# Hh blocks and gz pieces turned through DRAM ahead of their use, product sums ordered later, one w1 gradient piece moved

## The chip, the core and the metric

One Trainium2 chip, one of its cores. The metric is device time in microseconds (us) of one execution. The kernel computes in a single launch.

The engines named below: PE is TensorE, which multiplies matrices; DVE is VectorE; ACT is ScalarE; POOL is GpSimd; SP is SyncE. In this kernel SP and POOL issue all transfers between device memory (DRAM) and on-chip memory (SBUF). Each engine runs its own instructions in order, so an instruction that waits holds up those behind it on the same engine. SP's queue includes the transposing transfers (`dma_start_transpose`), which read a matrix from DRAM and leave its transpose in SBUF. POOL's queue has only plain and indexed transfers.

## The reference

The reference is the forward pass of one conditioned block and all its gradients. With S = 2048 tokens, D = 1024 and F = 3584:

```python
sa, ca, ga, sb, cb, gb = six rows of silu(c) @ w_mod
h = layernorm(x) * (1 + ca) + sa
x = x + ga * irfft2(rfft2(h) * (w_r + 1j * w_i))      # mixer over tokens and channels
h = layernorm(x) * (1 + cb) + sb
x = x + gb * (gelu(layernorm(h) @ w1 + b1) @ w2 + b2) # channel MLP
...
out, vjp = jax.vjp(forward, A_x, A_w_r, A_w_i, w1, b1, w2, b2, c, w_mod)
return out, *vjp(grad_out)
```

Ten outputs: the result, and the gradients of x, w_r, w_i, w1, b1, w2, b2, c and w_mod. The gradient of w2 is the product of the activated hidden values (Hh in this text, transposed) with gB, the output gradient scaled by gb. The gradient of w1 is the product of the normalized input with gz, the gradient at the hidden layer before its activation.

## The kernel before

The transforms are done as matrix products with cosine and sine matrices. All large products run on PE in 128x128 by 128x512 steps of bf16. The tokens are cut into NB = 4 blocks of BW = 512, the hidden size into NFC = 28 pieces of 128 rows (fc), or 7 groups of four (g). In order of time the kernel runs

1. the modulation rows, the product of the output gradient with w2 (ph) and the forward spectral part;
2. the MLP's forward pass (z_block, bo_pass). It also forms gz and stores Hh and gz to DRAM as d_hh and d_gz, both laid out hidden row by token;
3. the gradient passes: for each block b, two passes pg_pass(b, h) of 7 x 16 matmuls (L1083) that read gz (tiles gzr, eight slots filled by load_gz, L1059) and the transposed w1. They are followed by the layernorm backward on DVE and ACT (ln_bwd), the product pru of gradient and n2u (L192), and the column sums of both (sums3, L215) on PE. The block's gradient gn3 becomes d_gx in DRAM, issued on POOL (L1289), and is folded into fbuf for the spectral part. n3u, n2u and au are one-block loads on SP (L1244, L1246, L1299); n2u is then scaled by ACT (L507);
4. the backward spectral part (spectral_core), whose steps are pu (L524, L530), pcs (L569), pv (L639, L655) and po (L737), with DVE work (pairs) between them. PE's holes here are filled with pieces of the w2 gradient: gw2_product, one piece being 16 matmuls (L1214) for half of one fc. Each fc needs its block of Hh with the hidden index along the free side, so hh_load (L1371) loads it with a transpose from d_hh. From fc 8 on three slots serve in turn, and block fc + 2 is asked for when piece fc begins;
5. the four output quarters (consume_bwd), DVE work that ends in out_1, with pieces of the w1 gradient between them and after them (L1409). One piece is again 16 matmuls, and 8 pieces use one group of 512 gz rows, loaded with two transposes (gw1_load, L1360), one group ahead.

The pieces of steps 4 and 5 come from one generator, pieces(), 112 in all less the four done early; fill(n) takes the next n. The calls of fill at fixed places settle how many pieces stand between two steps of the spectral part. In consume_bwd quarter i first gets 6, 6, 8 or 8 pieces, then its column sum (accCA), then 2 more.

The order on each engine is decided by a scheduler at build time from dependences and estimated durations. `tc.issue_after(x)` and `behind(a, b)` are extra rules of order: the first puts what is inside it after x, the second puts a after b on the same engine without a wait. In pg_pass of a block b > 0 the sums of block b - 1 that are in `sums_in` (the first two token rows of both products) are put behind the matmul of step (g, i) = (2, 0):

```python
if b > 0 and h == 0 and (g, i) == (2, 0):
    for ins in sums_in:
        behind(ins, last_pg[0])
    sums_in.clear()
```

The gmod_ring steps (L1123 to L1137) work on the rows of the w_mod gradient beside step 4: loads of w_mod on SP, a reduction and a scaling on DVE, a store on POOL, through three buffers.

Of the kernel before, what the change touches and what calls it, by code (L numbers as in the profile page):

```python
# [11 lines left out]
BF16 = mybir.dt.bfloat16  # L12
# [5 lines left out]
P = 128  # L18
# [3 lines left out]
NT = S // P  # L22
# [9 lines left out]
BW = S // NB  # L32
# [3 lines left out]
def kernel(  # L36
# [24 lines left out]
    nc = tc.nc  # L61
# [4 lines left out]
    reg = ctx.enter_context(tc.tile_pool(name="reg", bufs=1))  # L66
    dram = ctx.enter_context(tc.tile_pool(name="dram", bufs=1, space=bass.MemoryType.DRAM))
# [44 lines left out]
    d_hh = dram.tile([F, S], BF16, name="d_hh")  # L112
    d_gz = dram.tile([F, S], BF16, name="d_gz")
    d_P = dram.tile([8, P, 4 * PW], BF16, name="d_P")
    d_SF = dram.tile([P, 4, 4, 512], BF16, name="d_SF")
    d_SI = dram.tile([P, 2, 4, 256], BF16, name="d_SI")
    d_E = dram.tile([P, 2, 8, 256], BF16, name="d_E")
    d_gmod = dram.tile([6 * D], BF16, name="d_gmod")
    d_ph_v = d_ph.rearrange("(fc p) s -> p fc s", p=P)
    d_hh_v = d_hh.rearrange("(fc p) s -> p fc s", p=P)  # L120
    d_gz_v = d_gz.rearrange("(fc p) s -> p fc s", p=P)
# [390 lines left out]
    def behind(ins, later):  # L512
        tc.add_manual_dep(ins.ins, later.ins.name, mybir.DependencyInfo(mybir.DependencyClass.NoSync, mybir.DependencyReason.DATA),
                          reason="order")
# [534 lines left out]
    gzs, g_sums, gn3s = {}, {}, {}  # L1049

    def gn3_of(b):
        if b % 2 not in gn3s:
            gn3s[b % 2] = reg.tile([P, 4, D], BF16, name=f"gn3{'ab'[b % 2]}", tag=("uv3", "wt")[b % 2])
        return gn3s[b % 2]

    def load_gz(b, g):
        n = b * 7 + g
        gzs[b, g] = gzr[n % 8 // 2][:, n % 2]
        nc.sync.dma_start(out=gzs[b, g], in_=d_gz_v[:, g * 4:(g + 1) * 4, b * BW:(b + 1) * BW])  # L1059

    def behind_w2(k):
        return tc.issue_after(w2_in[(NB - 1) * 14 + min(max(k, 0), 13)].ins)
# [1 line left out]
    for g in range(7):  # L1064
        wtile = reg.tile([P, 4, D], BF16, name=f"w1T_{g}", tag=W1T[g])
        for k in range(4):
            fc = g * 4 + k
# [4 lines left out]
            load_gz(0, g)  # L1072

    last_pg = [None]
    sums_in = []

    def pg_pass(b, h, pool, before=lambda: ExitStack()):
        pgs = [pool(k)("pg") for k in range(4)]
        for g in range(7):
            for i in range(4):  # L1080
                for k in range(4):
                    with before():
                        last_pg[0] = nc.tensor.matmul(pgs[i][:], lhsT=gzs[b, g][:, k, i * P:(i + 1) * P],  # L1083
                                                      rhs=w1Ts[g][:, k, h * KH:(h + 1) * KH],
                                                      start=(g == 0 and k == 0), stop=(g == 6 and k == 3))
                    last_pe[0] = last_pg[0]
                if b > 0 and h == 0 and (g, i) == (2, 0):
                    for ins in sums_in:
                        behind(ins, last_pg[0])
                    sums_in.clear()  # L1090
            for k in range(4 if b < 2 and h == 1 else 0):
                nc.scalar.activation(out=gzs[b, g][:, k, :], in_=gzs[b, g][:, k, :], func=ACT.Identity,  # L1092
                                     accum_out=gb1_acc[:, g * 4 + k, b:b + 1])
            if g < 6:
                yield
        for i in range(4):
            with tc.high_priority():
                nc.scalar.activation(out=gn3_of(b)[:, i, h * KH:(h + 1) * KH], in_=pgs[i][:], func=ACT.Identity,
                                     accum_out=g_sums[b][:, h, i:i + 1])
        yield  # L1100
# [90 lines left out]
    hh_in = [None]  # L1191
# [4 lines left out]
    def sums3(b, g4, p4):  # L1196
        for i in range(4):
            for j in range(4):
                src = (g4, p4)[j // 2][:, i, (j % 2) * KH:(j % 2 + 1) * KH]
                ins = strip_sum(acc3[0], j, src, b == 0 and i == 0, b == 3 and i == 3)  # L1200
                if b < 3 and i < 2:
                    sums_in.append(ins)

    def sums3_ga(b, p4):
        halves_sum(acc3[1], p4, b == 0, b == 3)
# [27 lines left out]
    def fold_quarter(b, ftmp, g2):  # L1233
# [3 lines left out]
        else:  # L1237
            fold2_in[b] = fold_pair(fbuf2[:, b], fbuf2[:, b - 1], ftmp, g2, ftmp[:, 0:2, :])

    for b in range(NB):  # L1240
        if b > 0:
            g_sums[b] = small.tile([P, 2, 4], FP32, name="sums", tag="sums")
# [7 lines left out]
        if b > 0:  # L1250
            for g in range(7):
                load_gz(b, g)
            if b == 2:
                hh_in_frame(0)
                hh_in_frame(1)
            for h in range(2):
                for _ in pg_pass(b, h, lambda k: ps_f):
                    pass
            with tc.issue_after(last_pg[0].ins):
                sums3_ga(b - 1, au)  # L1260
                if b == 2:
                    gb1_rows()
# [57 lines left out]
    hh_s = [hhp[:, 0], hhp[:, 1]] + [otl[:, k * NT * P:(k + 1) * NT * P].rearrange("p (t f) -> p t f", f=P) for k in range(2)] + \  # L1320
        [hht[k // 2][:, k % 2] for k in range(4)]
    hh_o = [None, None] + [4, 5, 6, 7, 4, 5] + [2, 0] + [1, 2, 0] * 6
# [4 lines left out]
    def consume_bwd(i, o4, tmp, tmp2, n1, eb):  # L1327
        if i == 0:
            accCA.append(ps_s("accCA"))
            nc.vector.tensor_copy(out=sacc, in_=eb[:, 0, :])  # L1330
        elif i == 2:
            tt(sacc, sacc, eb[:, 0, :], ALU.add)
        unfold_d(o4, tmp)
        unfold_tok(o4, tmp)
        load_tok(n1, A_x, i, nc.gpsimd)
        with tc.issue_after(last_po[0].ins):
            norm_act(n1, n1, 0, i)
        tt(tmp, o4, n1, ALU.mult)
        s1c = small.tile([P, 4], FP32, tag="s1c")
        for q in range(4):  # L1340
            t = 4 * i + q
            nc.vector.tensor_tensor_reduce(out=o4[:, q, :], in0=o4[:, q, :], in1=opca_row, scale=1.0, scalar=0.0,
                                           op0=ALU.mult, op1=ALU.add, accum_out=s1c[:, q:q + 1])
            ln_bwd(o4[:, q, :], s1c[:, q:q + 1], n1[:, q, :], stats[:, 0, 0, t:t + 1], o4[:, q, :], tmp2[:, q, :])
        nc.sync.dma_start(out=n1, in_=chunk_rows(d_gx1, i))
        tt(o4, o4, n1, ALU.add)
        store_tok(out_1, o4, i)
        fill((6, 6, 8, 8)[i])
        halves_sum(accCA[0], tmp, i == 0, i == 3)
        fill(2)  # L1350
        if i == 3:
            rows = small.tile([P, D], BF16, tag="gmrow", bufs=1)
            store_halves(accCA[0], rows[0:64, 0:KH], tmp, 1)


    w1g = {}

    def gw1_load(fg):
        for k in range(2):
            ins = nc.sync.dma_start_transpose(out=w1g["gz"][2 * (fg % 2) + k][:],  # L1360
                                              in_=d_gz[fg * 512:(fg + 1) * 512, k * 1024:(k + 1) * 1024])
        return ins
# [5 lines left out]

    def pieces():
        def hh_load(fc):  # L1370
            hh_in[0] = nc.sync.dma_start_transpose(out=hh_s[hh_o[fc]], in_=d_hh[fc * P:(fc + 1) * P, :])  # L1371

        for fc in range(2, 6):
            hh_load(fc)
# [45 lines left out]
    def fill(n):  # L1420
        for _ in range(n):
            next(todo)
        done[0] += n
# [86 lines left out]
```

## Time and profile before

| | |
|---|---|
| median of 3 runs | 1435.88 us |
| lowest, highest run | 1435.77, 1447.16 us |
| the profiled execution | 1443.81 us |
| its span, first to last instruction | 1441.9 us |
| mean granted clock of PE | 0.985 |
| moved by transfers | 321.68 MB, mean 223 GB/s |
| packets under 512 bytes | 207210 of 353505 |

How to read what follows. The views of the profile come from that one execution. In the view of stretches, each row gives a stretch of the span, its mean, then for PE, PE's weight loads, DVE, ACT and POOL the busy time with the number of instructions; the last three numbers are the granted PE clock, the share of the transfer engines that was busy (it can pass 1, since packets that wait for each other overlap) and the rate in GB/s. In a timeline, a row is a run of equal instructions: start, time from the first start to the last end, engine, line, operation, tiles; square brackets give the idle time before it and what ended that. In the chain of waits, a row is start, duration and what the end was waiting for at that time. In a list of waits a row names who waited, for whom, the sum in us, how often, and the longest.

### The profile page before, as it was taken

How to read it: one execution, taken by the hardware profiler on the slowest of the kernel's cores; microseconds unless marked ns; L12 is line 12 of the kernel's file. 1: busy time of each engine (PE TensorE's matmuls, PEld its weight loads, DVE VectorE, ACT ScalarE, POOL GpSimd, SP SyncE). 2: the span in 40 equal slices, each digit the busy share in tenths (PEclk: the TensorE clock that was granted, in tenths of full speed). 3: DMA queues.
4: the chain of work that ended last, by engine and by line, in shares of the span. 5: the costliest groups of instructions: out<-in, count | busy, mean ns of one | idle time of the engine just before them, and what ended most of it. 6: DMA issues, size and time to landing. Idle time of an engine off the chain costs nothing. (4 is left out here: it accounts for less than half of the span.)

```text
span 1441.9 us, 18528 instructions
## 1 busy us (share of the span) xinstructions
PE 1369.0 (95%) x6838; PEld 663.5 (46%) x6963; DVE 1072.4 (74%) x1505; ACT 743.9 (52%) x1061; POOL 372.1 (26%) x468
## 2 busy tenths in 40 slices
PE   5999999999999999999999999999997999899996
PEld 2445674444444444444444444444443574444443
DVE  5898889987798886877412999997566859898532
ACT  4775766657987766666117654343422455333111
POOL 5601622201112112221210001202344532232322
PEclk8999999999999999999999999999999999999998
DMA  9963647999687876887998446475999998656993
GB/s 331 296 219 100 171 133 241 270 309 325 204 259 241 244 235 220 253 272 208 307 290 170 146 161 234 168 190 161 231 229 229 251 241 219 194 164 182 280 222 121
DMA packets 353505, 321.68 MB, mean 223 GB/s; under 512 B 207210, under 2 KB 296832, under 8 KB 353286
## 3 DMA queue, kind: packets, MB, share of 16 engines
q1 hardware_dynamic: 317510, 199.84, 53.7%
q0 software_dynamic: 35904, 120.65, 24.8%
q8 instruction: 54, 0.88, 0.3%
q14 instruction: 37, 0.30, 0.1%
HBM read 161.01 MB, written 110.15 MB: 188 GB/s over the span
## 5 line engine op out<-in xcount | busy, mean ns | idle before, releaser
L803 PE MATMUL pp<-gBoT,wt 128*128 128x512 bf16 x874 | 195.2, 379 | 4.5 <-DVE phr L809 1.5
L1083 PE MATMUL pg<-w1T,gzr 128*128 128x512 bf16 x877 | 195.7, 381 | 1.0
L1409 PE MATMUL gw1acc<-gzh,n3n 128*128 128x512 bf16 x876 | 194.2, 379 | 1.1
L1083 PEld LDWEIGHTS <-gzr 128*128 128x128 bf16 x896 | 87.3, 98 | 108.3 <-issue 5.6
L928 PEld LDWEIGHTS <-w 128*128 128x128 bf16 x896 | 87.3, 98 | 107.3 <-issue 2.9
L803 PEld LDWEIGHTS <-wt 128*128 128x128 bf16 x896 | 87.4, 98 | 107.0 <-issue 4.4
L1409 PEld LDWEIGHTS <-n3n 128*128 128x128 bf16 x896 | 87.5, 98 | 104.9 <-issue 1.3
L1214 PE MATMUL gw2acc<-gB,hhsA 128*128 128x512 bf16 x406 | 94.4, 388 | 10.5 <-DMA hhsA<-d_hh 9.8
L928 PE MATMUL pz<-n3Ta,w 128*128 128x512 bf16 x439 | 98.2, 379 | 1.9 <-ACT gt L931 1.5
L928 PE MATMUL pz<-n3Tb,w 128*128 128x512 bf16 x436 | 98.0, 379 | 0.7 <-issue 0.2
L985 PEld LDWEIGHTS <-hhA 128*128 128x128 bf16 x608 | 59.0, 98 | 72.7 <-issue 2.5
L931 ACT ACTIVATE gt<-pz,b_col 128x512 bf16<-128x512 f32 x112 | 73.0, 685 | 34.6 <-PE pz L928 34.2
L1221 ACT CAST gwo<-gw2acc 128x512 bf16<-128x512 f32 x46 | 26.6, 583 | 114.4 <-DMA out_dram<-gwo 50.4
L1413 ACT CAST gwo<-gw1acc 128x512 bf16<-128x512 f32 x47 | 27.4, 584 | 109.8 <-PE gw1acc L1409 98.2
L942 ACT ACTIVATE gt<-gt 128x2048 bf16<-128x2048 bf16 x28 | 53.5, 1910 | 59.2 <-DVE gt L192 59.2
L192 DVE TENSOR_TENSOR gt<-gt,gt 128x2048 bf16<-128x2048 bf16 x56 | 68.5, 1224 | 20.6 <-ACT gt L944 19.4
L192 DVE TENSOR_TENSOR ct<-ct 128x2048 bf16<-128x2048 bf16 x68 | 80.6, 1216 | 3.6 <-DMA d_n<-ct 2.9
L1214 PEld LDWEIGHTS <-hhsA 128*128 128x128 bf16 x416 | 41.2, 100 | 61.0 <-DMA hhsA<-d_hh 11.0
L1134 DVE CUSTOM_DVE_ANT_0 otl<-otl 128x1024 bf16<-128x1024 bf16 x24 | 29.1, 1222 | 51.0 <-DMA otl<-in_w_mod_dram 46.3
L938 ACT ACTIVATE gt<-gt 128x2048 bf16<-128x2048 bf16 x28 | 53.5, 1910 | 1.8 <-DVE w2sA L192 1.0
L944 ACT ACTIVATE gt<-gt 128x2048 bf16<-128x2048 bf16 x28 | 53.4, 1908 | 0.4
L1414 POOL DMA_DIRECT2D out_dram<-gwo x56 | 30.9, 553 | 86.2 <-ACT gwo L1413 44.1
(343 smaller groups left out, 2544.0 us busy)
## 6 DMA issues: line engine op xcount, KB each, us to landing
gzr<-d_gz SPq DMA_DIRECT2D x28, 512.0 KB
wblk<-in_w_mod_dram SPq DMA_DIRECT2D x12, 1024.0 KB
out_dram<-otl POOLq DMA_DIRECT2D x48, 256.0 KB
out_dram<-gwo POOLq DMA_DIRECT2D x96, 128.0 KB
d_ph<-pho POOLq DMA_DIRECT2D x21, 512.0 KB
d_hh<-hhA POOLq DMA_DIRECT2D x19, 512.0 KB
w<-in_B_w_dram SPq DMA_DIRECT2D x7, 1024.0 KB
hhC<-d_ph SPq DMA_DIRECT2D x14, 512.0 KB
```

Of the source, the lines that this page charges most:

```text
L192: return nc.vector.tensor_tensor(out=out, in0=a, in1=b, op=op)
L803: last_pe[0] = nc.tensor.matmul(pp[:], lhsT=wt[:, fg % 2, cch, k * P:(k + 1) * P], rhs=gBoT[j][:, cch, :], start=(cch == 0), stop=(cch == ...
L928: last_pe[0] = nc.tensor.matmul(pz[:], lhsT=w1s[g][:, cch, k * P:(k + 1) * P], rhs=n3T[:, cch, :], start=(cch == 0), stop=(cch == NDC - 1))
L931: z_in = nc.scalar.activation(out=zb[:, k, :], in_=pz[:], func=ACT.Identity, bias=b1_col[:, fc:fc + 1], scale=1.0)
L938: nc.scalar.activation(out=av, in_=zb, func=ACT.Square)
L942: nc.scalar.activation(out=sg, in_=bv, func=ACT.Sigmoid, scale=2.0 * GK)
L944: nc.scalar.activation(out=bv, in_=bv, func=ACT.Sigmoid, scale=-2.0 * GK)
L985: last_pe[0] = nc.tensor.matmul(pbs[i][:], lhsT=hh[:, k, i * P:(i + 1) * P], rhs=wp[:, k, :], start=False, stop=(g == 6 and k == 3))
L1083: last_pg[0] = nc.tensor.matmul(pgs[i][:], lhsT=gzs[b, g][:, k, i * P:(i + 1) * P], rhs=w1Ts[g][:, k, h * KH:(h + 1) * KH], start=(g == 0 ...
L1214: nc.tensor.matmul(acc[:], lhsT=hh_of(fc)[:, t, :], rhs=gBs[t // 4][:, t % 4, h * KH:(h + 1) * KH], start=(t == 0), stop=(t == NT - 1))
L1409: nc.tensor.matmul(acc[:], lhsT=n3ns[t // 4][:, t % 4, cch * P:(cch + 1) * P], rhs=gz2[t // 8][:, t % 8, :], start=(t == 0), stop=(t == NT ...
L1414: nc.gpsimd.dma_start(out=out_4[cch * P:(cch + 1) * P, fg * 512:(fg + 1) * 512], in_=ob)
```

## The change

Two DRAM tensors are added, d_hhT for twelve blocks of Hh (fc 10 to 21) and d_gzT for the first 512 rows of gz in four pieces. While blocks 1 and 2 of the gradient passes run, six blocks of Hh each are loaded with a transpose on SP into one of two SBUF buffers (hb) and stored as they stand by POOL. While block 3 runs, four gz pieces are turned in the same way. The turns of a block may be issued once its last gz load is. Later, hh_load for those fc and gw1_load for the first group read the turned data with plain transfers.

The sums of block b - 1 are split in two lists: those of gn3 stay behind step (2, 0), those of pru go behind step (4, 2). And quarter 1 gets 3 pieces behind its column sum where it got 2.

```diff
+    d_hhT = dram.tile([12, P, NT * P], BF16, name="d_hhT")
+    d_gzT = dram.tile([4, P, NT * P], BF16, name="d_gzT")
...
-        nc.sync.dma_start(out=gzs[b, g], in_=d_gz_v[:, g * 4:(g + 1) * 4, b * BW:(b + 1) * BW])
+        gz_in[0] = nc.sync.dma_start(out=gzs[b, g], in_=d_gz_v[:, g * 4:(g + 1) * 4, b * BW:(b + 1) * BW])
...
-    sums_in = []
+    sums_in = [[], []]
...
-                if b > 0 and h == 0 and (g, i) == (2, 0):
-                    for ins in sums_in:
+                if b > 0 and h == 0 and (g, i) in ((2, 0), (4, 2)):
+                    for ins in sums_in[g // 4]:
                         behind(ins, last_pg[0])
-                    sums_in.clear()
+                    sums_in[g // 4].clear()
...
                 if b < 3 and i < 2:
-                    sums_in.append(ins)
+                    sums_in[j // 2].append(ins)
...
+    turned = [0]
+
+    def turn(dst, src, mm):
+        hb = reg.tile([P, mm, NT * P // mm], BF16, name="hb", tag=("gm", "sb")[turned[0] % 2])
+        turned[0] += 1
+        nc.sync.dma_start_transpose(out=hb[:], in_=src)
+        nc.gpsimd.dma_start(out=dst, in_=hb[:].rearrange("p a b -> p (a b)"))
...
             for g in range(7):
                 load_gz(b, g)
+            if b < 3:
+                for fc in range(4 + 6 * b, 10 + 6 * b):
+                    with tc.issue_after(gz_in[0].ins):
+                        turn(d_hhT[fc - 10], d_hh[fc * P:(fc + 1) * P, :], NT)
+            else:
+                for k in range(4):
+                    with tc.issue_after(gz_in[0].ins):
+                        turn(d_gzT[k], d_gz[0:512, k * 512:(k + 1) * 512], 4)
...
-        fill(2)
+        fill(3 if i == 1 else 2)
...
         for k in range(2):
+            if fg == 0:
+                ins = nc.sync.dma_start(out=w1g["gz"][k][:].rearrange("p (j a) b -> p j (a b)", j=2),
+                                        in_=d_gzT[2 * k:2 * k + 2].rearrange("j p n -> p j n"))
+                continue
...
-            hh_in[0] = nc.sync.dma_start_transpose(out=hh_s[hh_o[fc]], in_=d_hh[fc * P:(fc + 1) * P, :])
+            if 10 <= fc < 22:
+                hh_in[0] = nc.sync.dma_start(out=hh_s[hh_o[fc]].rearrange("p a b -> p (a b)"), in_=d_hhT[fc - 10])
+            else:
+                hh_in[0] = nc.sync.dma_start_transpose(out=hh_s[hh_o[fc]], in_=d_hh[fc * P:(fc + 1) * P, :])
```

1 line of the change is left out of this document (added).

## The prediction

> **What bounds the kernel now.** I read the page's head first, then the stretches of time, then the list of what TensorE (PE) waited for, and last the chain of waits and the engines' own timelines where PE stood still.
>
> ```profile
> span 1441.9 us, 18528 instructions
> PE 1369.0 (95%) x6838; PEld 663.5 (46%) x6963; DVE 1072.4 (74%) x1505; ACT 743.9 (52%) x1061; POOL 372.1 (26%) x468
> ...
> 840.00:880.00 40.00, 37.72 (x176) 16.47 (x177) 36.05 (x48) 16.37 (x20) 1.59 (x2) 0.96 0.47 161
> 880.00:920.00 40.00, 38.47 (x192) 17.00 (x195) 37.28 (x61) 14.76 (x24) 2.59 (x2) 1.00 0.40 138
> 920.00:960.00 40.00, 39.79 (x188) 17.90 (x191) 38.73 (x44) 15.85 (x22) 10.15 (x6) 1.00 0.89 262
> ...
> 1040.00:1080.00 40.00, 36.78 (x184) 18.05 (x187) 25.95 (x36) 11.26 (x20) 17.16 (x23) 1.00 1.11 240
> 1080.00:1120.00 40.00, 31.72 (x146) 14.89 (x148) 25.87 (x38) 9.48 (x16) 18.91 (x24) 0.91 1.09 222
> ...
> 1240.00:1280.00 40.00, 34.83 (x179) 17.77 (x181) 36.89 (x49) 16.68 (x21) 10.59 (x13) 0.91 0.56 158
> ...
> PE gw2acc L1214 <- DMA hhsA<-d_hh: 9.8, 3, 3.8
> PE po L737 <- ACT eb L742: 5.0, 1, 5.0
> PE acc3a L215 <- DVE pru L192: 4.0, 3, 2.1
> PE pu L530 <- DVE fbuf L192: 3.8, 2, 2.5
> ```
>
> PE is busy 95% of the span, so the end moves only where a hole in PE closes. In the table of stretches the first number after PE is its busy time of 40 us. Three places of the second half have holes: 840 to 920 (37.72 and 38.47), 1040 to 1120 (36.78 and 31.72), and 1240 to 1280 (34.83). In 1080:1120 and 1240:1280 the granted clock also falls, to 0.91. The waits name the causes: transposed Hh loads (hhsA), the copy of eb on ACT, the product pru on DVE, and later DVE's fbuf. The change touches all four.
>
> One caution on the base. The sum is made against the profiled execution: 1441.9 us of span, 1443.81 us in all. The runs shown are 1435.77, 1435.88 and 1447.16, so it lies 7.9 above their median. Either that is a constant of profiling, or this execution had more of the stalls below than the runs near the median. No view tells which, so I carry half, 4 us.
>
> **Part A: twelve Hh blocks (fc 10 to 21) are loaded plain, not transposed.** In the backward spectral stretch PE repeats a unit: one pcs group of 16 matmuls and four gw2 products.
>
> ```profile
> 1038.30 1.91 PE L569 MATMUL pcs<-empf,U 128*128 128x256 bf16 x16
> 1053.86 1.91 PE L569 MATMUL pcs<-empf,U 128*128 128x256 bf16 x16
> 1072.02 1.91 PE L569 MATMUL pcs<-empf,U 128*128 128x256 bf16 x16
> 1088.35 1.91 PE L569 MATMUL pcs<-empf,U 128*128 128x256 bf16 x16
> 1094.09 8.77 PE L1214 MATMUL gw2acc<-gB,hhsA 128*128 128x512 bf16 x31 [3.83 <-DMA hhsA<-d_hh]
> 1110.39 1.91 PE L569 MATMUL pcs<-empf,U 128*128 128x256 bf16 x16
> ...
> 1131.46 7.61 PE pv L639 x64
> 1139.08 1.75 PE pcs L569 x16
> ...
> 817.93 3.85 DMA gzr<-d_gz
> 1041.04 17.01 DMA hhsA<-d_hh
> 1064.65 9.83 DMA otl<-d_hh
> 1091.56 11.87 DMA otl<-d_hh
> 1103.49 12.26 DMA hhsA<-d_hh
> ```
>
> A unit without a wait is 1053.86 - 1038.30 = 15.56 us. The next ones take 18.16, 16.33, 22.04 and, with the 7.61 of pv taken out, 1139.08 - 7.61 - 1110.39 = 21.08. The excess is 2.60 + 0.77 + 6.48 + 5.52 = 15.4 us. It holds the waits and the slow clock behind them (the 31 matmuls at 1094.09 need 8.77 us). Each unit uses two blocks in order, and the one from 1053.86 uses fc 12 and 13, so all these waits are for blocks among the twelve.
>
> The four loads on the chain took 9.83 to 17.01 us from issue to use, for 512 KB. A plain load of 512 KB, gzr at 817.93, took 3.85. With twice that (7.7), for a queue that other traffic shares, the four would be 9.3, 2.1, 4.2 and 4.6 us earlier. The largest single waits are 3.8, so nearly all of it goes. With three times (11.6) the last two gain 0.3 and 0.7 and most of their 12.0 us stays. I take 14 us. The ends are 5 and 15.4. I stay near the upper end because the queue itself is relieved: the twelve transposes leave it. What is late next? PE itself: the unit from 1038.30 kept 15.56 us with the same DVE and ACT work beside it, so the pair chain can hold that pace.
>
> The Trainium skill speaks against this part. Its page "Advanced Engine Details and Errata", section "X-Bar Transpose (TRN2)", says that transposing transfers are as fast as regular ones. By that page part A would be 0 and the time 1434. The trace differs, 9.83 to 17.01 against 3.85, though not under the same load; hence the first rival below.
>
> **Part B: the third output quarter.** Before its po matmuls PE waits 5.0 us.
>
> ```profile
> 1255.00 5.14 PE po L737 x28
> 1170.19 13.97 PE pv L655 x128
> ...
> 1226.82 2.29 DVE L192 TENSOR_TENSOR ct<-ct,xt 128x4096 bf16<-128x4096 bf16 x1 [3.20 <-DMA xt<-d_gx]
> 1206.71 13.64 SPq L1360 DMA_TRANSPOSE gzh<-d_gz  x3
> 1220.53 0.45 SPq L1345 DMA_DIRECT2D xt<-d_gx  x1
> ```
>
> The wait ends when ACT copies eb, and ACT stands behind a scaling (L1178) that needs DVE; DVE in turn had stood 3.20 us for xt<-d_gx. That load was issued at 1220.53, straight behind three gz transposes that held SP for 13.64 us. Two edits meet here. One more w1 gradient piece, 16 matmuls at (15.56 - 1.75)/64 = 0.216 from the unit of part A, puts 3.5 us of PE work into the 5.0; it is taken from the tail, so PE's total stays. And the first two gz pieces become plain loads, so only one transpose stands ahead of xt, which can take up to 3.2 us from DVE. Behind the wait the 28 narrow matmuls took 5.14 us, where 13.97/128 each makes 3.1: 2.0 us of slow clock. So B is worth 3.5 (only the piece fits, the clock still drops) to 7.0. I take 6. The slots of SP behind it keep their order.
>
> **Part C: the sums later, and sixteen turns in the gradient passes.** PE's three waits for pru are 4.0 us. The changed order on PE puts the pru sums behind 40 matmuls of pg in each block, where they stood behind 31, 28 and 23: 9, 12 and 17 later, 1.9, 2.6 and 3.7 us at 0.216. The longest wait is 2.1, so they all go if DVE keeps its time. But DVE sets the pace here.
>
> ```profile
> 889.20 1.22 DVE L1174 CUSTOM_DVE_ANT_0 got<-gn3a,n3u 128x1024 bf16<-128x1024 bf16 x1
> 941.82 1.22 DVE L1174 CUSTOM_DVE_ANT_0 got<-gn3b,n3u 128x1024 bf16<-128x1024 bf16 x1
> 988.47 1.23 DVE L1134 CUSTOM_DVE_ANT_0 otl<-otl 128x1024 bf16<-128x1024 bf16 x1 [3.94 <-DMA otl<-in_w_mod_dram]
> ...
> 871.69 6.63 DMA d_gx<-gn3b
> 819.64 0.82 POOL L1289 DMA_DIRECT2D d_gx<-gn3a  x1 [66.31 <-ACT gzr L1092]
> 872.83 4.64 ACT L507 ACTIVATE n2u<-n2u,stats 128x1024 bf16<-128x1024 bf16 x4 [5.33 <-DMA n2u<-d_x]
> 886.82 0.60 ACT L1098 ACTIVATE gn3a<-pg 128x512 bf16<-128x512 f32 x1 [9.36 <-PE pg L1083]
> 770.57 17.61 SPq L1059 DMA_DIRECT2D gzr<-d_gz  x7
> 836.16 0.45 SPq L1299 DMA_DIRECT2D au<-d_A  x1
> 931.39 15.65 SPq L1371 DMA_TRANSPOSE hht<-d_hh  x4
> ```
>
> The first DVE operation of block 2 (889.20) and of block 3 (941.82) shows no idle time before it: DVE came from the block before, 52.6 us of its own work. In 880:960 it is busy 76 of 80 us. So PE, 4.0 us sooner, would stand 4 us longer at fbuf (where it waits 3.8 already). The gain reaches the path only through DVE's own wait, 3.94 at 988.47, for w_mod behind two transposes on SP; in the changed order one of those two goes out earlier. Upper end: 3.9.
>
> Against it stand the turns. A turn is a transpose on SP and a store on POOL; two buffers serve them all. Each third turn waits on SP for the store of the first, with n3u, n2u, au and the gz loads queued behind. Four transposes in a row took 15.65 us, 3.9 each; a store of 1 MB, d_gx, took 6.63, so one of 512 KB costs 3.3 to 6.6. A buffer's cycle is then 3.9 + 3.3 = 7.2 to 10.5 us, and six turns, three cycles, 22 to 32. In the first block they begin before the last of the seven gz loads that hold SP from 770.57 to 788.2, by about 786, and should be through at 808 to 818, ahead of d_gx at 819.64, which stands behind the six stores on POOL. In the second they begin about where SP now issues au, 836.16, into a full queue, add some 8 us, and end at 866 to 876, across d_gx at 871.69. The chain has DVE's fold waiting for the end of that store at 878.3, so 0 to 6 us of delay go straight onto DVE's chain. n2u has more room: ACT ended with it at 877.5 and next waited until 886.82, 9.4 us. The four gz turns fall into the stretch with DMA 0.40. Bandwidth is there: 16 turns are 63 us of transposing, and the stretches 840:920 leave 45 of 80 us free.
>
> So C lies between +3.9 and -6; I take 0, near its middle. A + B + C = 14 + 6 + 0 = 20: 1443.8 - 20 = 1424, less the 4: **1420 us**.
>
> **The rivals.**
> 1. The loads are late because the queue is full, and a plain load in it is as late. For it: DMA stands at 1.11 and 1.09 in 1040:1120. Against: the transposes are part of that fullness. A is then 0, and 1443.8 - 6 - 4 = 1434.
> 2. Slower: the turns block POOL and SP. Place: d_gx of blocks 0 and 1, and through it DVE's fold. It decides when a buffer's cycle exceeds (819.64 - 786)/3 = 11 us; from there each us costs 3 per block. At the 17.01 of a crowded transpose plus 6.63, a cycle is 23.6, six turns 71, and two blocks lose 37 each: 1443.8 + 74 - 20 - 4 = 1494. At 16 us a cycle it is 14 each, 1449. For it: one transpose did need 17.01. Against: the DMA queues are half idle here (0.47, 0.40).
> 3. Everything goes right: A 15.4, B 7, C 3.9, and the 7.9 is a constant of profiling: 1435.9 - 26.3 = 1410.
>
> **How the numbers follow.** Forecast 0.55, rival 1 0.20, rival 2 0.12, rival 3 0.13. The forecast's own range goes from A 15.4, B 7 and the whole 7.9, 1413, to A 5 and B 3.5, 1443.8 - 8.5 - 4 = 1431. About 1% either way is what a measurement of this kernel can tell from no change; that is 1421.5 and 1450.2. Below 1421.5 lie rival 3 and two thirds of the forecast, 0.13 + 0.37 = 0.50. Above 1450 lies half of rival 2, 0.06, and the rest, 0.44, is within. The range has to take in the forecast with C down to -6 (1437), rival 1 and most of rival 3: 1407 to 1438. It leaves out most of rival 2 and the edges of the others, some 0.17.
>
> **What would show it.** Right in A: pcs groups 15.6 us apart from 1038 to 1131, no PE wait for hhsA, DMA clearly under 1.0 there. Right in B: no wait before the 28 po matmuls, clock 1.00. Right in C: no PE wait for pru, d_gx of block 1 issued by 875. A DVE wait of several us for d_gx, or PE standing over 4 us at fbuf, would prove C worse; PE waits for hhsA after plain loads would mean rival 1. A gain well over 26 us, or any loss, makes the prediction wrong.

## The result, and the profile after

| | before | after |
|---|---|---|
| median | 1442.68 us (22 runs) | 1437.37 us (22 runs) |
| lowest, highest run | 1431.09, 1456.66 | 1431.46, 1441.31 |
| profiled execution, its span | 1443.81, 1441.9 | 1436.28, 1434.5 |

The ratio is 0.996, with a 95% interval from 0.9941 to 0.9979: some 5 us less, where I had forecast 20 us against the profiled base. The time lies inside my range, the size of the step does not fit.

First the head of the page, after.

```profile
span 1434.5 us, 18708 instructions
PE 1376.4 (96%) x6963; PEld 663.9 (46%) x6963; DVE 1070.7 (75%) x1504; ACT 743.8 (52%) x1062; POOL 379.1 (26%) x484
```

And from the list of waits, after, the largest of PE between 780 and 1020 us:

```profile
PE pu L532 <- DVE fbuf L194: 6.4, 1, 6.4
PE acc3a L217 <- DVE gn3a L1183: 6.0, 1, 6.0
PE pg L1087 <- ACT gn3b L1102: 4.2, 3, 2.1
```

No wait for hhsA is left, and none over 0.6 us for pru. In their place stand waits for DVE and ACT inside the gradient passes (L1183 is their layernorm backward), and the one at fbuf has grown from 2.5 to 6.4 us. The stretches after, in the columns of the table in the prediction:

```profile
840.00:880.00 40.00, 39.44 (x186) 17.13 (x185) 36.32 (x56) 15.49 (x28) 4.84 (x9) 0.97 0.91 261
880.00:920.00 40.00, 34.02 (x162) 14.34 (x161) 29.02 (x43) 13.37 (x17) 4.64 (x7) 0.91 0.94 283
920.00:960.00 40.00, 38.21 (x183) 16.95 (x181) 31.86 (x41) 13.47 (x24) 8.27 (x5) 1.00 0.77 223
1040.00:1080.00 40.00, 40.00 (x211) 20.47 (x210) 32.91 (x48) 13.22 (x23) 23.66 (x26) 1.00 0.85 273
1080.00:1120.00 40.00, 40.00 (x211) 20.45 (x210) 33.46 (x48) 12.71 (x22) 27.46 (x32) 1.00 0.98 298
1240.00:1280.00 40.00, 35.93 (x193) 17.98 (x192) 36.69 (x50) 15.88 (x20) 9.93 (x14) 1.00 0.61 167
```

The spectral stretch (1040 to 1120) is now full: PE 40.00 of 40 us, clock 1.00. But 880:920, where DVE was busy 37.28 us and set the pace, shows DVE at 29.02: it stands still there. The transfer engines went from 0.47 and 0.40 to 0.91 and 0.94 in 840:920.

The whole difference can be cut at a few marks that both traces have: the first DVE operation of each block in the gradient passes (got<-gn3a or gn3b, n3u), the first and the last of the eight pcs groups, PE's last matmul and the end of the span.

```profile
784.29 1.23 DVE L1178 CUSTOM_DVE_ANT_0 got<-gn3a,n3u 128x1024 bf16<-128x1024 bf16 x1 [32.41 <-ACT gn3a L1102]
839.38 1.22 DVE L1178 CUSTOM_DVE_ANT_0 got<-gn3b,n3u 128x1024 bf16<-128x1024 bf16 x1
900.00 1.22 DVE L1178 CUSTOM_DVE_ANT_0 got<-gn3a,n3u 128x1024 bf16<-128x1024 bf16 x1
957.21 1.22 DVE L1178 CUSTOM_DVE_ANT_0 got<-gn3b,n3u 128x1024 bf16<-128x1024 bf16 x1
...
1039.96 1.91 PE L571 MATMUL pcs<-empf,U 128*128 128x256 bf16 x16
1156.30 1.91 PE L571 MATMUL pcs<-empf,U 128*128 128x256 bf16 x16
1429.68 0.22 PE L209 MATMUL ptr<-fin,gc_bf 128*8 128x128 bf16 x1
```

And the marks before that the prediction does not show:

```profile
783.03 1.23 DVE L1174 CUSTOM_DVE_ANT_0 got<-gn3a,n3u 128x1024 bf16<-128x1024 bf16 x1 [32.41 <-ACT gn3a L1098]
835.37 1.22 DVE L1174 CUSTOM_DVE_ANT_0 got<-gn3b,n3u 128x1024 bf16<-128x1024 bf16 x1
...
1022.74 1.91 PE L569 MATMUL pcs<-empf,U 128*128 128x256 bf16 x16
1154.47 1.91 PE L569 MATMUL pcs<-empf,U 128*128 128x256 bf16 x16
1430.41 0.22 PE L207 MATMUL ptr<-fin,gc_bf 128*8 128x128 bf16 x1
```

| stage | before | after | difference |
|---|---|---|---|
| up to block 0 on DVE | 783.03 | 784.29 | +1.26 |
| block 0 to 1 | 52.34 | 55.09 | +2.75 |
| block 1 to 2 | 53.83 | 60.62 | +6.79 |
| block 2 to 3 | 52.62 | 57.21 | +4.59 |
| block 3 to the first pcs | 80.92 | 82.75 | +1.83 |
| first to last pcs group | 131.73 | 116.34 | -15.39 |
| last pcs to PE's last matmul | 275.94 | 273.38 | -2.56 |
| PE's last matmul to the end | 11.49 | 4.82 | -6.67 |
| the span | 1441.9 | 1434.5 | -7.40 |

Part A gave 15.4 us, and the gradient passes took 17.2 back before it began. PE ends only 0.7 us sooner. The rest, 6.67 us, comes from behind PE's last instruction, where I had looked for nothing:

```profile
1431.44 0.54 POOL L1414 DMA_DIRECT2D out_dram<-gwo  x1 [2.91 <-ACT gwo L1413]
```

```profile
1430.71 0.54 POOL L1441 DMA_DIRECT2D out_dram<-gwo  x1 [2.91 <-ACT gwo L1440]
```

These are the last stores on POOL, before and after. The span runs 10.5 us beyond the first and 3.8 us beyond the second. In the raw records, which the views leave out here because the instruction does no work, POOL's closing DRAIN lasts 9.71 us before and 3.02 us after, and every engine waits for it.

What was late in the gradient passes is told by the chain of waits, after, through block 1 (start, duration, what was waited for):

```profile
839.80 7.06 DMA hb<-d_hh
846.90 0.51 issue
847.42 5.07 DMA d_hhT<-hb
852.50 6.51 DMA hb<-d_hh
859.05 0.48 issue
859.53 5.53 DMA d_hhT<-hb
865.08 7.83 DMA hb<-d_hh
...
879.34 9.78 DMA d_gx<-gn3b
889.21 2.37 DVE gn3b L194 x2
```

Transpose, store, transpose, store: the turns of one buffer stand in series, 839.80 to 852.50 to 865.08, 12.6 us a cycle. On POOL the sixth store and d_gx follow on it. The last store and d_gx of blocks 0 and 1 on POOL, and DVE's waits for d_gx (the timeline, after):

```profile
818.57 0.53 POOL L1250 DMA_DIRECT2D d_hhT<-hb  x1 [1.16 <-DMA hb<-d_hh]
820.88 0.77 POOL L1309 DMA_DIRECT2D d_gx<-gn3a  x1 [1.78 <-ACT gzr L1096]
...
878.80 0.55 POOL L1250 DMA_DIRECT2D d_hhT<-hb  x1
879.34 0.77 POOL L1309 DMA_DIRECT2D d_gx<-gn3b  x1
...
829.87 2.36 DVE L194 TENSOR_TENSOR gn3a<-pru 128x2048 bf16<-128x2048 bf16 x2 [2.81 <-DMA d_gx<-gn3a]
889.21 2.36 DVE L194 TENSOR_TENSOR gn3b<-pru 128x2048 bf16<-128x2048 bf16 x2 [8.23 <-DMA d_gx<-gn3b]
```

The same two DVE operations before:

```profile
825.86 2.36 DVE L192 TENSOR_TENSOR gn3a<-pru 128x2048 bf16<-128x2048 bf16 x2
...
878.41 2.36 DVE L192 TENSOR_TENSOR gn3b<-pru 128x2048 bf16<-128x2048 bf16 x2 [0.54 <-DMA d_gx<-gn3b]
```

In block 0 d_gx is not late. It leaves 36.6 us behind the block's first DVE operation in both kernels (819.64 before, 820.88 after). But DVE could go on 6.2 us after its issue before, without a wait, and 9.0 us after it now: the store lands later, right behind the last stores of the turns. In block 1 d_gx left at 871.69 before and leaves at 879.34 now. Of these 7.65 us the block brought 4.01 with it, since it began later (839.38, not 835.37); 3.64 are the wait behind the stores on POOL. The store then needs 9.78 us where it took 6.63. The two, 3.64 and 3.15, are the 6.79 by which the step grew.

### The profile page after: what moved, and what is told of

It is laid out like the page before. It is cut to its first block, busy times and chain, and to the rows that moved or that the text cites. A ratio compares the mean times of both kernels' runs of the same rounds, so it can differ in the third digit from the quotient of the medians.

```text
span 1434.5 us, 18708 instructions
## 1 busy us (share of the span) xinstructions
PE 1376.4 (96%) x6963; PEld 663.9 (46%) x6963; DVE 1070.7 (75%) x1504; ACT 743.8 (52%) x1062; POOL 379.1 (26%) x484
## 3 DMA queue, kind: packets, MB, share of 16 engines
q1 hardware_dynamic: 319846, 208.23, 54.3%
## 5 line engine op out<-in xcount | busy, mean ns | idle before, releaser
L1087 PE MATMUL pg<-w1T,gzr 128*128 128x512 bf16 x896 | 199.7, 384 | 4.7 <-ACT gn3b L1102 4.2
L944 ACT ACTIVATE gt<-gt 128x2048 bf16<-128x2048 bf16 x28 | 53.5, 1910 | 59.1 <-DVE gt L194 59.1
L940 ACT ACTIVATE gt<-gt 128x2048 bf16<-128x2048 bf16 x28 | 53.5, 1910 | 1.7 <-DVE w2sA L194 1.1
L946 ACT ACTIVATE gt<-gt 128x2048 bf16<-128x2048 bf16 x28 | 53.4, 1908 | 0.4
L1218 PE MATMUL gw2acc<-gB,otl 128*128 128x512 bf16 x224 | 50.0, 379 | 0.0
```

The costliest lines, as they stand in the source:

```text
L940: nc.scalar.activation(out=av, in_=zb, func=ACT.Square)
L944: nc.scalar.activation(out=sg, in_=bv, func=ACT.Sigmoid, scale=2.0 * GK)
L946: nc.scalar.activation(out=bv, in_=bv, func=ACT.Sigmoid, scale=-2.0 * GK)
L1218: nc.tensor.matmul(acc[:], lhsT=hh_of(fc)[:, t, :], rhs=gBs[t // 4][:, t % 4, h * KH:(h + 1) * KH], start=(t == 0), stop=(t == NT - 1))
```

## The experiments

All kernels run against the kernel before on the same chip; their ratios are to it, as recorded, and are not the quotients of the medians shown. Beside the experiments the median of the kernel before was 1444.49, 1442.37 or 1446.78 us, so a difference of a few us between the medians of two rows is to be read with care. The table sums the runs up; all but the median and the ratio comes from one profiled execution of each kernel. The steps are those of DVE from block to block, then the time from the first to the last pcs group, PE's last matmul, the time from the last store on POOL to the end of the span, the DMAs that POOL issues, and the timed result.

| kernel | 0-1 | 1-2 | 2-3 | pcs | PE's last | to the end | DMAs | median us | ratio (95%) |
|---|---|---|---|---|---|---|---|---|---|
| before | 52.3 | 53.8 | 52.6 | 131.7 | 1430.4 | 10.5 | 410 | 1442.68 | |
| after | 55.1 | 60.6 | 57.2 | 116.3 | 1429.7 | 3.8 | 426 | 1437.37 | 0.996 (0.9941 to 0.9979) |
| no turns | 53.3 | 52.8 | 58.4 | 116.1 | 1419.0 | 10.5 | 410 | 1432.33 | 0.9897 (0.9843 to 0.995) |
| turns only | 54.3 | 60.9 | 53.3 | 126.8 | 1436.2 | 3.8 | 426 | 1442.2 | 0.9974 (0.9948 to 1.0) |
| sums and piece | 52.3 | 53.4 | 58.3 | 127.8 | 1428.6 | 10.5 | 410 | 1444.76 | 0.9998 (0.9956 to 1.004) |
| six turns | 53.0 | 52.7 | 57.1 | 122.7 | 1426.1 | 3.4 | 416 | 1430.25 | 0.9868 (0.9814 to 0.9921) |
| six stores, early | 52.9 | 53.0 | 52.6 | 125.1 | 1440.0 | 3.4 | 416 | 1455.96 | 1.0102 (1.0073 to 1.013) |
| sums, d_gx first | 53.0 | 52.8 | 53.1 | 132.4 | 1433.0 | 10.5 | 410 | 1444.27 | 1.001 (0.9987 to 1.0032) |
| d_gx before turns | 52.6 | 53.8 | 58.9 | 116.3 | 1418.6 | 3.8 | 426 | 1426.61 | 0.9875 (0.9817 to 0.9932) |
| both orders | 53.1 | 53.8 | 53.9 | 116.1 | 1415.5 | 3.8 | 426 | 1421.95 | 0.9855 (0.9796 to 0.9915) |
| six stores, late | 52.9 | 53.0 | 53.4 | 135.7 | 1436.3 | 3.4 | 416 | 1437.05 | 0.9926 (0.9891 to 0.9961) |
| twelve turns | 52.9 | 54.8 | 53.5 | 116.1 | 1419.3 | 3.7 | 422 | 1423.34 | 0.9835 (0.979 to 0.988) |
| both orders, old sums | 53.2 | 56.7 | 53.3 | 116.1 | 1416.4 | 3.8 | 426 | 1426.17 | 0.9884 (0.9833 to 0.9935) |
| six turns, d_gx first | 53.1 | 52.8 | 53.7 | 123.3 | 1427.1 | 3.4 | 416 | 1430.19 | 0.9874 (0.9826 to 0.9922) |

**No turns.** The turns go; the loads stay plain and read rows of d_hh as they stand.

```diff
...
-                    with tc.issue_after(gz_in[0].ins):
-                        turn(d_hhT[fc - 10], d_hh[fc * P:(fc + 1) * P, :], NT)
...
-                    with tc.issue_after(gz_in[0].ins):
-                        turn(d_gzT[k], d_gz[0:512, k * 512:(k + 1) * 512], 4)
...
-                                        in_=d_gzT[2 * k:2 * k + 2].rearrange("j p n -> p j n"))
+                                        in_=d_hh[2 * k * P:(2 * k + 2) * P, :].rearrange("(j p) n -> p j n", p=P))
...
-                hh_in[0] = nc.sync.dma_start(out=hh_s[hh_o[fc]].rearrange("p a b -> p (a b)"), in_=d_hhT[fc - 10])
+                hh_in[0] = nc.sync.dma_start(out=hh_s[hh_o[fc]].rearrange("p a b -> p (a b)"), in_=d_hh[fc * P:(fc + 1) * P, :])
```

> The changed kernel without its sixteen turns. The twelve Hh blocks and the first two gz pieces are loaded plain from rows of d_hh that were never turned, the same bytes at the same places, so the w2 gradient of these blocks and the first w1 gradient piece come from other data; the sums' order and the extra piece stay. Theory (the turns cost the gradient passes some 16 us: PE's first pu behind them went from 1000.9 to 1016.7): pu back at 1000 to 1003, the time 16 us below the changed kernel, 1418 to 1424. Rival (the sums' new order or the plain loads' own place cost it): pu still near 1016 and the time within 4 us of 1437.

Neither held. PE waits at fbuf until 1005.70 (1016.73 after), and its last matmul came 10.7 us sooner than after, not 16. Block 1 to 2 is whole again at 52.8, but 2 to 3 is still 58.4. And the median fell by 5.0 us, less than PE's end, since the end behind POOL's last store is 10.5 us again. So the turns are not the only cost, and the kernel after had been flattered by its short end.

**Turns only.** The loads, the sums and the pieces as before; the turns are made and not read.

```diff
...
+            if b < 3:
+                for fc in range(4 + 6 * b, 10 + 6 * b):
+                    with tc.issue_after(gz_in[0].ins):
+                        turn(d_hhT[fc - 10], d_hh[fc * P:(fc + 1) * P, :], NT)
+            else:
+                for k in range(4):
+                    with tc.issue_after(gz_in[0].ins):
+                        turn(d_gzT[k], d_gz[0:512, k * 512:(k + 1) * 512], 4)
...
```

> The kernel before, with the sixteen turns made and never read: all loads transposed as before, sums in the old order, two pieces ahead of the third quarter. Theory (the turns alone cost the gradient passes 16 us and nothing later gives it back): pu near 1017, 1456 to 1460. Rival (the cost is in the sums' order): within 3 us of the kernel before, 1440 to 1446.

The time is far from 1456 and within the rival's range, but not for the rival's reason. The turns do cost: 54.3 and 60.9 us for the steps 0-1 and 1-2. The step 2-3 is 53.3, so the four gz turns cost nothing there. PE's last matmul comes 5.8 us later than before, and the short end takes 6.7 off.

**Sums and piece.** The two small edits without any turn.

```diff
-                if b > 0 and h == 0 and (g, i) == (2, 0):
+                if b > 0 and h == 0 and (g, i) in ((2, 0), (4, 2)):
...
-        fill(2)
+        fill(3 if i == 1 else 2)
```

> The kernel before with the two small edits alone: the pru sums behind 40 matmuls of pg, and three pieces ahead of the third quarter; no turn, all loads transposed. Theory: DVE sets the pace of the gradient passes, so the sums' order gives nothing there (pu at 999 to 1002), and the piece fills 2.5 to 3.5 us of the wait for eb: 1439 to 1441. Rival (the sums' order is what cost 16 us): pu at 1010 or later, 1450 to 1460.

Neither: the time is that of the kernel before, and PE's first pu behind the gradient passes comes at 1003.68 (1000.92 before). But here the other loss shows alone: step 2-3 takes 58.3 us. The timeline of DVE in this kernel:

```profile
919.20 2.29 DVE L192 TENSOR_TENSOR gB<-got,rows 128x4096 bf16<-128x4096 bf16 x1
921.40 2.29 DVE L192 TENSOR_TENSOR gn3a<-gn3a,got 128x4096 bf16<-128x4096 bf16 x1
...
935.69 2.36 DVE L192 TENSOR_TENSOR gn3a<-pru 128x2048 bf16<-128x2048 bf16 x2 [7.47 <-DMA d_gx<-gn3a]
```

and of POOL and SP in the same kernel:

```profile
922.41 3.52 POOL L1334 MEMSET cs01b<- 128x4112 bf16 x1 [41.69 <-PE pg L1085]
925.88 0.80 POOL L1299 DMA_DIRECT2D d_gx<-gn3a  x1
...
925.83 3.81 SPq L1308 DMA_DIRECT2D gB<-d_gB  x2
```

The kernel before has the two DVE operations in the other order:

```profile
921.35 2.29 DVE L192 TENSOR_TENSOR gn3a<-gn3a,got 128x4096 bf16<-128x4096 bf16 x1
923.56 2.28 DVE L192 TENSOR_TENSOR gB<-got,rows 128x4096 bf16<-128x4096 bf16 x1
...
930.28 2.36 DVE L192 TENSOR_TENSOR gn3a<-pru 128x2048 bf16<-128x2048 bf16 x2
```

The sum that d_gx stores is gn3a<-gn3a,got. With the pru sums in their new place the scheduler put the product for gB ahead of it, and POOL's clearing of cs01b ahead of d_gx. Counted from the block's first DVE operation (885.71, before 889.20) the sum ends after 38.0 us where it ended after 34.4; 2.2 of these 3.6 us are the product ahead of it. d_gx comes another 1.7 us later (it leaves 2.2 us behind the sum's end at 923.69; before it left at 924.18, 0.5 behind). It now goes out at the same moment as two gB loads of 1 MB (925.83), which before came 3.35 us behind it (927.53). DVE can go on 9.8 us after its issue; before, DVE found it landed at 930.28, at most 6.1 us after. The diff does not show this swap anywhere.

**Six turns.** Two in each of blocks 1 to 3, one for each buffer.

```diff
-                for fc in range(4 + 6 * b, 10 + 6 * b):
...
+            for fc in range(12 + 2 * b, 14 + 2 * b):
...
-            if 10 <= fc < 22:
+            if 14 <= fc < 20:
```

> The changed kernel with six turns in place of sixteen: Hh blocks 14 to 19, two in each of blocks 1 to 3 of the gradient passes, one for each buffer, so that none waits for a store; blocks 10 to 13, 20, 21 and all gz pieces are loaded transposed. Theory (the cost comes from the cycle of transpose, store and next transpose, 12.6 us for a pair, three cycles a block): with one cycle a block d_gx keeps its place, pu at 1001 to 1005, and of part A some 10 to 12 us stay, 1428 to 1434. Rival (each turn costs its share of 16 us wherever it stands): pu near 1007, 1434 to 1438.

The places are those of the theory: pu at 1004.09, and the steps 0-1 and 1-2 whole (53.0 and 52.7: two turns a block cost nothing there). Of part A's 15.4 us 9.0 stay, not 10 to 12, and the step 2-3 has the swap again. The 1430.25 us lie in the forecast range, but with 7.0 us of the short end, which the theory did not count.

**Six stores, early and late.** The end behind POOL's last store went with the turns in every kernel so far, and so with the number of DMAs on POOL. The kernel before gets six small stores and nothing else. In the first kernel they run at 16.6 to 22.7 us; in the second they stand behind d_gx of block 2, at 923.5 to 926.1.

```diff
+        if b == 0:
+            for k in range(6):
+                nc.gpsimd.dma_start(out=d_dum[k], in_=ones_bf[:, 0:64])
```

> The kernel before with six extra small stores on POOL (128x64 of ones to an unused DRAM tile, early in the program); nothing else changes. In the profiled executions the span ends 10.5 us behind the issue of the last store on POOL wherever the kernel makes no turns (the kernel before 1431.44 of 1441.9, no turns 1420.03 of 1430.5, sums and piece 1429.62 of 1440.1), and 3.4 to 3.8 us behind it wherever it does (the changed kernel 1430.71 of 1434.5, turns only, six turns). Theory (the end's length hangs on how many DMAs POOL has issued, not on the turns' work): 3.4 to 3.8 us here, the time 6.7 us below the kernel before, ratio 0.995 to 0.996. Rival (it hangs on the turns, or is chance): 10.5 us, ratio 1.000.

> The kernel before with the same six small stores, now behind d_gx of block 2 on POOL, where the first try had them at the program's start and lost some 15 us in the forward stages. Theory (POOL's closing drain, 9.7 us with 410 DMAs and 2.4 to 3.0 with 416 or 426, hangs on the count alone): the span ends 3.4 to 3.8 us behind the last store on POOL; PE's last matmul within 3 us of 1430; the time 6.7 us below the kernel before, ratio 0.995 to 0.996. Rival (the drain is short in some executions whatever the kernel, and the timed runs do not have it): ratio 1.000.

Placed at the start, they upset the forward stages (PE waits 13.7 us for one load of wt, and DVE begins block 0 at 798.75), so the time says nothing; but the end is 3.4 us long. Placed late they leave the forward stages alone (block 0 begins at 781.86), and the end is 3.4 us again. PE's last matmul comes at 1436.26, outside the 3 us around 1430, since the spectral stretch with its transposed loads took 135.7 us in this execution. The ratio is 0.9926, whose interval holds the 0.9954 of 6.7 us. So the gain is there in timed runs too, with no turn made. The length goes with the count of POOL's DMAs: 410 give 9.7 us of closing drain in four kernels, 416 to 426 give 2.4 to 3.0 in ten. Where between 410 and 416 it changes, and why, is not shown.

**Sums, d_gx first.** Sums and piece, with two rules of order.

```diff
-        tt(g2[:], g2[:], go4, ALU.add)
-        nc.gpsimd.dma_start(out=chunk_rows(d_gx1, b), in_=g2[:])
+        add = tt(g2[:], g2[:], go4, ALU.add)
+        gx_in[b] = nc.gpsimd.dma_start(out=chunk_rows(d_gx1, b), in_=g2[:])
...
-            tt(gBs[2][:], go4, bcn(gb_row, 4), ALU.mult)
+            with tc.issue_after(add.ins):
+                tt(gBs[2][:], go4, bcn(gb_row, 4), ALU.mult)
...
-    nc.gpsimd.memset(css2[:], 0.0)
+    with tc.issue_after(gx_in[2].ins):
+        nc.gpsimd.memset(css2[:], 0.0)
```

> Sums and piece alone (no turns), with two order edges in block 2: DVE's product for gB stays behind the sum that d_gx stores, and POOL's memset of cs01b behind d_gx. Theory (in sums and piece alone, blocks 2 to 3 took 58.3 us in place of 52.6 on DVE, because the scheduler put that product ahead of the sum: d_gx left 2.2 us later, the memset added 1.7, and the two gB loads then went out with it, so that it took 9.8 us and not 6.1): block 2 to 3 back at 52.5 to 53.5 us, pu at 998 to 1000, some 4 to 5 us below sums and piece. Rival (the sums matmuls themselves, later on PE, delay DVE): 57 to 58 us, no gain.

The step 2-3 is back at 53.1: the two swaps were the cause, not the sums' matmuls. Which of the two edges did it is not separated. The gain of 4 to 5 us did not come: the median of ten runs is 1444.27, against 1444.76 of sums and piece. In the profiled execution block 0 began at 787.21, 7.2 us later than in sums and piece, and the spectral stretch with its transposed loads took 132.4 us in place of 127.8; one execution can't say why the median stayed.

**d_gx before turns.** The kernel after, with the last two of six stores in blocks 1 and 2 behind d_gx.

```diff
-                    with tc.issue_after(gz_in[0].ins):
+                    with tc.issue_after(gz_in[0].ins), tc.issue_after(gx_in[b - 1].ins) if fc >= 8 + 6 * b else ExitStack():
                         turn(d_hhT[fc - 10], d_hh[fc * P:(fc + 1) * P, :], NT)
```

> The changed kernel with the last two of six turns in blocks 1 and 2 behind d_gx of the block before on POOL: four stores stand ahead of d_gx, not six. The transposes keep their places on SP. Theory (d_gx is late because its issue stands behind the serial cycle of two buffers): d_gx of block 1 issued at 870 to 874 in place of 879.3, DVE's step from block 1 to 2 at 54 to 56 us in place of 60.6, the time 4 to 6 us below the changed kernel, 1431 to 1433. Rival (the traffic of the turns slows d_gx and the other transfers wherever it stands): the step stays at 59 us or more, and the time within 2 us of 1437.

POOL and DVE of this kernel, in blocks 0 and 1:

```profile
817.79 0.76 POOL L1310 DMA_DIRECT2D d_gx<-gn3a  x1 [15.93 <-ACT gzr L1097]
824.00 2.36 DVE L194 TENSOR_TENSOR gn3a<-pru 128x2048 bf16<-128x2048 bf16 x2
...
860.77 0.53 POOL L1251 DMA_DIRECT2D d_hhT<-hb  x1 [5.38 <-DMA hb<-d_hh]
869.74 0.76 POOL L1310 DMA_DIRECT2D d_gx<-gn3b  x1 [8.44 <-issue]
872.58 0.55 POOL L1251 DMA_DIRECT2D d_hhT<-hb  x1
...
876.88 2.36 DVE L194 TENSOR_TENSOR gn3b<-pru 128x2048 bf16<-128x2048 bf16 x2 [0.94 <-DMA d_gx<-gn3b]
```

In block 1 d_gx leaves at 869.74, 36.0 us behind the block's start where it left 40.0 behind it, and DVE waits 0.94 us where it waited 8.23; the step 1-2 is 53.8, as before the change. In block 0 d_gx leaves at its old place, and DVE goes on 6.2 us after it without a wait, as before the change. All twelve Hh turns are still made in the same blocks, and all their transposes are still issued ahead of d_gx. So what cost was the order of the stores on POOL, which held d_gx back in block 1 and slowed its landing in both blocks, and not the turns' traffic wherever it stands. The median is 10.8 us below that of the kernel after, more than the 4 to 6 expected; in the profiles the steps 0-1 and 1-2 make 9.3 us, and block 0 also begins 3.1 us sooner.

**Both orders.** The two edits above together, in the kernel after.

> The changed kernel with both repairs: the last two of six turns behind d_gx, and in block 2 the gB product behind the sum and the memset behind d_gx. Theory (the two orders are separate costs, 5 us each): DVE's steps 54, 55 and 53 us, pu at 1005 to 1008, part A whole, PE's last matmul at 1419 to 1421 and the time 1424 to 1428. Rival (once d_gx is on time, n2u or the loads behind the transposes on SP are late next): pu at 1012 or later, 1430 to 1434.

The median, 1421.95 us, is the lowest of the study, with a ratio of 0.9855 (twelve turns, below, has 0.9835; the intervals overlap). The steps are 53.1, 53.8 and 53.9, part A is whole, and PE ends at 1415.5, some 4 us sooner than expected. The step 2-3 is 5.0 us shorter than in d_gx before turns, and PE's last matmul 3.1 us sooner. In the median the second repair gives 4.7 us here, with overlapping intervals, and 0.5 and 0.1 us in the two other pairs (sums and piece, six turns); its worth in time is not shown. What is late next is n2u, whose load stands behind the transposes on SP: ACT waits 17.75 us for it in block 1, and DVE then 1.59 us for ACT.

**Twelve turns; old sums; six turns with d_gx first.** Each is both orders but for one part: without the four gz turns; with the pru sums in their old place; with six turns in place of sixteen, where d_gx needs no rule and only that of block 2 stays.

> The changed kernel with both repairs, without the four gz turns: the first two gz pieces are loaded transposed again, the twelve Hh turns stay. Theory (the plain gz loads give part B nothing, since xt<-d_gx made DVE wait 2.5 us with them and 1.9 without; only the extra piece counts): 1420 to 1424, as with all sixteen. Rival (they relieve SP ahead of xt<-d_gx, as I forecast): 2 to 4 us later, 1424 to 1426.

> The changed kernel with both repairs and the pru sums in their old place, behind 31, 28 and 23 matmuls of pg. Theory (DVE sets the pace of the gradient passes, so the sums' place on PE is worth 0 to 1 us): PE waits some 4 us for pru, pu within 1.5 us of 1004, 1420 to 1424. Rival (those waits are on the path): 4 us later, 1425 to 1427.

> Six turns (Hh blocks 14 to 19) with the order edges of block 2. Theory: the gradient passes lose nothing (DVE's steps 53, 53 and 53.5 us), but the transposed loads left among the twelve still cost PE 3 to 7 us in the spectral stretch: 1425 to 1428, behind the twelve turns. Rival (six turns cover all that was late): 1420 to 1423.

Without the gz turns the time is the same within the intervals, though PE waits 3.4 us for eb (2.1 with them): from the last pcs group to PE's last matmul it takes 274.6 us without them and 273.0 with them. The old place of the sums is undecided: PE waits 7.0 us for pru, the longest 4.3, and ends 1.0 us later in the profile, but the median is 4.2 us higher and the intervals overlap. Its step 1-2 took 56.7 us, since DVE stood 4.1 us for d_gx of block 1, though that store left on time (35.6 us behind the block's start): with the repaired order too it can land late, and why it did here was not traced. Six turns give the steps that were expected, and lose 7.3 us in the spectral stretch; the time came 2 us above what I had put down.

## Why the prediction was wrong, point by point

**Part A was right.** The pcs groups stand 15.56 us apart (1039.96, 1055.52, ...), no wait for hhsA, the transfer share 0.85 and 0.98 where it was 1.11 and 1.09 (the second is hardly "clearly under 1.0"); 15.4 us against my 14. Rival 1 falls. The page "Advanced Engine Details and Errata" of the Trainium skill, section "X-Bar Transpose (TRN2)", would have made this zero; the trace does not agree: the same bytes at the same places, loaded plain, remove all of the 15.4 us, with turns (after) and without (no turns). Whether the transfers themselves are faster, or SP, is not separated: between 1015 and 1160 us the issue of one hhsA load takes SP 2.9 to 8.4 us when it transposes (before) and 0.3 to 0.4 us when it is plain (after).

**Part B was too large.** From the last pcs group to PE's last matmul it gave 2.6 us, not 6. The clock stayed at 1.00 and the piece fits, but the gz turns hardly moved xt<-d_gx: DVE waits 2.50 us for it after, 3.20 before, and 1.93 in sums and piece, where all gz loads are transposed:

```profile
1227.68 2.29 DVE L194 TENSOR_TENSOR ct<-ct,xt 128x4096 bf16<-128x4096 bf16 x1 [2.50 <-DMA xt<-d_gx]
```

```profile
1226.53 2.29 DVE L192 TENSOR_TENSOR ct<-ct,xt 128x4096 bf16<-128x4096 bf16 x1 [1.93 <-DMA xt<-d_gx]
```

So PE still stands 2.49 us ahead of the 28 po matmuls: of the two signs the clock came, the end of the wait did not.

**Part C is the step that failed,** in two places: the price of the turns, and a change of order that the sum left out.

The first is the sentence "A buffer's cycle is then 3.9 + 3.3 = 7.2 to 10.5 us". It is 12.6 us (7.06 + 5.07, 6.51 + 5.53, with the issues between). I took the 3.9 from four transposes in a row, 15.65 us. That is a rate: in a row they overlap. After, two transposes issued at 797.84 and 799.96 had their stores at 803.47 and 805.40, some 5.5 us later each and 1.9 apart. In a chain, where each waits for a store and the store waits for it, what counts is the time from issue to landing of a single one, 6.5 to 7.8 us in this busy stretch. So six turns took not 22 to 32 but 39 us (839.80 to 878.80) up to the issue of the last store. I had named the right victim, "across d_gx(1)", with 0 to 6 us, and then took the middle of C: POOL held d_gx back by 3.64 us, it landed 3.15 us slower, and the step grew by 6.8.

For the first block the forecast put nothing, because the six turns would be through ahead of d_gx. They were issued ahead of it (818.57, d_gx at 820.88), but a store that is issued is not yet landed: d_gx left on time, but DVE stood 2.81 us for its landing where it had not waited before, and the step grew by 2.75. The slowing of one store by those right ahead of it was a term that the sum did not have. The experiment with d_gx ahead of the last two stores takes back 6.8 and 2.5.

The second was not in my sum at all. The edit of the sums changed the order of two DVE operations and of a POOL clearing in block 2, some 5 us (4.6 after, 5.7 in sums and piece). In the kernel after, the clearing costs nothing more (d_gx leaves 0.5 us behind the sum, as before); there the sum ends 3.5 us later in the step, and DVE goes on 10.7 us after d_gx's issue (938.52, the same moment as the two gB loads at 938.47). I had followed the sums' own matmuls on PE, and not what else the scheduler moved. It fixes the order on DVE and POOL at build time, so both swaps stood there ahead of any run.

So C was not 0 but about -17, of which 14.1 lie in the three steps; 1.3 of the rest stand ahead of block 0, where single profiles of these kernels differ by 7 us, and 1.8 between block 3 and the first pcs group were not traced. The signs that were to prove C worse all came: d_gx after 875, DVE waiting 8.23 us for it, PE over 4 us at fbuf. The last of them says little, since both orders, without these losses, has 4.9 us there too: PE without its waits for pru is early. (Of the 3.8 us for fbuf that the prediction read, 2.5 stand here, the rest in the forward part.) The waits for pru went as forecast, and gave nothing that the path shows, as DVE set the pace.

**Rival 2 had the mechanism** and the point from which it decides, a cycle over 11 us, but its price began at 16 us a cycle. At 12.6 its own rule gives 3 x 1.6 = 5 us a block, 10 in all, where 2.75 and 6.79 were measured. That the sum is near is in part luck: in block 0 the turns were issued in time and the cost came from the landing.

**The caution on the base** put the profiled execution 7.9 us above the median of the first three runs; over 22 runs the median is 1442.68, 1.1 below it. So of the 4 us taken off only 1.1 were there.

**Not foreseen:** 6.7 us at POOL's end. Without them the change would have shown 0.7 us in the profile. With both orders kept, 1421.95 was measured where 1420 was forecast, but that nearness is luck: 6.7 us of it are the short end, part A gave 15.7, part B 3.0, and the steps still cost 2.1.

## What to carry to other kernels

A transfer that stands in a serial chain is priced by its time from issue to landing, not by its share of a row of overlapping ones. On a queue in order the important store waits for the issue of all that stand ahead of it, and here it also landed some 3 us later right behind them; so put the store that the next stage needs ahead of the work that has time. When a scheduler orders the instructions, compare the order on every engine, not just on the one that the edit names: a rule for one matmul moved a product and a memset on two other engines. And look behind the last matmul too, before a small gain is put down to the change.

## What was not expected of the hardware

POOL's closing drain took 9.70 to 9.71 us in the four kernels with 410 DMAs on POOL (before among them), and 2.38 to 3.04 us in the ten with 416, 422 or 426. It was the same to 0.01 us over the four. What sets it was not found.

With transposed loads of the twelve Hh blocks the time from the first to the last pcs group ranged from 125.1 to 135.7 us over six kernels (before, turns only, sums and piece, sums with d_gx first, and both with six stores), one profile each; with plain loads from 116.1 to 116.3 over six. So the transposed loads cost 9 to 20 us in these executions. The runs of the kernel before spread over 25.6 us and those of the kernel after over 9.9; that the transposed loads are the reason is likely but not shown, since turns only, which has them too, spreads over 7.5 us in ten runs.
